# A Fourier mixing layer and an ELU feed-forward block on one core: one product, the middle x sums and the special-row copies change places

## The chip, the cores and the metric

The kernel runs on one core of one Trainium2 chip. The metric is the time of one execution on the device in microseconds, lower is better. The engines that matter are TensorE (PE in the profile; PEld is its weight load), VectorE (DVE), ScalarE (ACT), GpSimd (POOL), and SyncE (SP), which here only issues DMAs.

## The reference

```python
def _attn_ref(x, filt_r, filt_i):            # x: 8 x 3008 x 256
    X = np.fft.rfft(x, axis=1)
    F = (filt_r + 1j * filt_i)[None, :, :]   # 1505 x 256
    return np.fft.irfft(X * F, n=x.shape[1], axis=1)

def _moe_ref(x, w_in, w_out):                # 24064 x 256, 256 x 2048, 2048 x 256
    h = x @ w_in
    g = np.where(h > 0.0, h, np.exp(np.minimum(h, 0.0)) - 1.0)
    return g @ w_out
```

The output of the first, as 24064 rows, is the input of the second. All is in 32-bit floats; the filters and weights arrive as 64-bit floats.

## The kernel before

The transform of 3008 = 47 x 64 is done as matmuls with tables. Each batch goes through five stages: x sums and first transform (`x_unit` L216, `a_unit` L226: chunks c = 0 to 5, two chunks to one `a_unit`, result z written to DRAM by `z_write` and read back by `z_read`), second transform (`b_unit` L374, for groups g = 0, 2, 4, 6), product with the filter (`re_mult`, `re_sums`, `im_mult` L415, `im_join` L421, `im_sums` L425), back transform (`bi_unit`, `y_write` to DRAM) and last transform (`y_read`, `n_unit`). The feed-forward block takes the result in 6 column blocks of a batch; for each block it goes through 4 quarters of the hidden width. One such quarter is called a quad: 8 x 6 x 4 = 192 quads, of about 13 us each.

A quad holds seven up steps (products with `w_in`, a Strassen-like scheme, so that seven products do the work of eight, with sums on VectorE between them) and the seven down steps (products with `w_out`) of the quad before. An up step writes into PSUM tiles called phs, pha and phd. The second phd product of a quad (`s4`) adds onto the bank that VectorE has to read first (`s7`: `add` at L538). After these come the exponential on ScalarE (`elu_exp`, L547 and L548) and the maximum on VectorE (`elu_max`, L552).

The mixing of batch b runs beside the feed-forward block of batch b - 1, in its 24 quads, counted 0 to 23 in this text. A dictionary `plan` says which function is called in which quad, and at one of three places: place 2 behind the third step of the quad, place 0 behind the eighth (or seventh), place 1 at the quad's end, behind the sums that close its up and down steps. Each engine works off its own instructions in the order in which these calls issue them. TensorE's order of up (U) and down (D) steps is `UUDUDDU` + place 0 + `DUUDUDD`, and, for quads in the set `opens`, `DUUDUDDU` + place 0 + `DUUDUD`: the quad then begins with a down step. `opens` holds the quads behind a unit that has taken all four shared PSUM banks.

These four banks (list `banks`) go round among all stages: a unit takes the first of the list, and returns it when its readers have been issued. `b_unit` takes four, called c, s, ci and si in it, and returns them in the order c, si, s, ci. ScalarE copies c and si into tile r (L387); for group 0 it also copies one special row group of all four banks, 32 partitions x 256, into a spare filter buffer (L390); VectorE then forms sums and differences with s and ci (L392, L393).

In the order before, the plan puts: `x_unit` and `a_unit` of chunks 0 and 1, 2 and 3, 4 and 5 into quads 0, 2 and 4 (batch 1: 2, 3 and 4), sums at place 0, matmuls, copies, the loads of later chunks (`x_load`) and `z_write` at place 1; `f_read` of two groups at quads 4, 8, 12, 16, place 1, and `z_read` at quads 5, 9, 13, 17, place 0; `b_unit` at the end of quads 6, 10, 14, 18; the real products in the quad behind it, the four imaginary products one quad later at place 2 and `im_join` at that quad's end; `im_sums` and `bi_unit` in the quad behind that. Last transforms (`n_unit`) lie in quads 23, 1, 5, 8, 12, 16; the tables and y for the one of quad 5 are read at quad 3, place 0. Output sums of a block (`c_unit`, `o_unit`, L628, L651) lie in quads 1 and 2, 5 and 6, and so on to 21 and 22.

The chunks' tiles rotate: x in four buffers, their sums (`sd`, L219) in two, the result of the first transform (`t1`, L237) in three.

Of the kernel before, what the change touches and what calls it, by code (L numbers as in the profile page):

```python
# [14 lines left out]
ALU = mybir.AluOpType  # L15
# [115 lines left out]
def kernel(  # L131
# [9 lines left out]
    nc = tc.nc  # L141
# [6 lines left out]
    def pool(name, bufs, **kw):  # L148
        return ctx.enter_context(tc.tile_pool(name=name, bufs=bufs, **kw))
# [42 lines left out]
    def bank(name, shape=(P, 2, D)):  # L192
        i = banks.pop(0)
        return i, psM.tile(list(shape), FP32, tag="m%d" % i, name=name)
# [179 lines left out]
    def b_unit(b, g):  # L374

        pf = [bank("pf") for _ in range(4)]
        both = [(a, p, slice(1 if g == a == 0 else 0, 2), 0) for a in range(4) for p in range(4)]
        if g == 0:
            both = [(0, p, slice(0, 1), 1) for p in range(4)] + both
        for a, p, js, v in both:  # L380
            r = slice(32 * p, 32 * p + 24)
            nc.tensor.matmul(pf[p][1][32 * a:32 * a + 32, js, :], fb[r, v, :], t2[r, js, a, :],  # L382
                             start=True, stop=True, tile_position=(32 * p, 32 * a))
        t = rs[b, g] = sp.tile([P, 4, 2, D], FP32, tag="r", name="r")
        c, s, ci, si = (ps for _, ps in pf)
        for k, ps in ((1, c), (3, si)):
            nc.scalar.activation(out=t[:, k], in_=ps, func=AXT.Copy)  # L387
        if g == 0:
            for k, ps in ((0, c), (2, si), (1, s), (3, ci)):
                nc.scalar.activation(out=once_in[0:32, k], in_=ps[0:32, 0, :], func=AXT.Copy)  # L390
        for k, ps in ((0, s), (2, ci)):
            nc.vector.tensor_tensor(out=t[:, k], in0=t[:, k + 1], in1=ps, op=ALU.add)  # L392
            nc.vector.tensor_tensor(out=t[:, k + 1], in0=t[:, k + 1], in1=ps, op=ALU.subtract)  # L393
        banks.extend(pf[p][0] for p in (0, 3, 1, 2))
# [17 lines left out]
        if g == 0:  # L412
            nc.gpsimd.tensor_copy(out=z[0:32, 0:2, 0, :], in_=z[0:32, 2:4, 0, :])

    def im_mult(b, g, c):  # L415
        t, f = rs[b, g], fall[:, 0:2]
        nc.vector.tensor_tensor(out=t[:, c], in0=t[:, c], in1=f[:, :, 1, c, :], op=ALU.mult)
        nc.vector.tensor_tensor(out=t[:, 2 + c], in0=t[:, 2 + c], in1=f[:, :, 0, c, :], op=ALU.mult)  # L418

    def im_join(b, g):  # L420
        t = rs[b, g]  # L421
# [355 lines left out]
    with tc.manual_schedule():  # L777
# [108 lines left out]
        op = pool("op", 1)  # L886
# [9 lines left out]
        def at(quad, place, fn, *a):  # L896
            plan.setdefault((quad, place), []).append((fn, a))
# [13 lines left out]
        for b in range(B):  # L911
            t = (b - 1) * PER
            if b > 0:
                for c, s in enumerate((2, 2, 3, 3, 4, 4) if b == 1 else (0, 0, 2, 2, 4, 4)):
                    at(t + s, 0, x_unit, b, c)
                    if c % 2 == 0:
                        opens.add(t + s + 1)
                        at(t + s, 1, a_unit, b, c)
                    nb, nxt = (b, c + XBUFS) if c + XBUFS < NXC else (b + 1, c + XBUFS - NXC)
                    if nb < B:  # L920
                        at(t + s, 1, x_load, nb, nxt)
                    at(t + s, 1, z_write, b, c)
                for g in range(0, NG, 2):
                    s = t + 6 + 2 * g
                    opens.update((s + 1, s + 4))
                    for k in (g, g + 1):
                        at(s - 2, 1, f_read, b, k)
                        at(s - 1, 0, z_read, b, k)
                    at(s, 1, b_unit, b, g)
                    at(s + 1, 2, re_mult, b, g)  # L930
                    at(s + 1, 1, re_sums, b, g)
                    for c in range(2):
                        at(s + 2, 2, im_mult, b, g, c)
                    at(s + 2, 1, im_join, b, g)
                    at(s + 3, 2, im_sums, b, g)
                    at(s + 3, 1, bi_unit, b, g)
                    at(s + 3, 1, y_write, b, g)
            for m, (s, place) in enumerate(((23, 0), (25, 1), (29, 1), (32, 0), (36, 0), (40, 0))):
                if b > 0 or m > 0:
                    at(t + s - 2, 0, tn_read, b, m)  # L940
                    at(t + s - 2, 1 if m == 0 else 0, y_read, b, m)
                    at(t + s, place, n_unit, b, m)

                    at(*((t + s + 1, 1) if m > 2 else (t + s, place)), n_sums, b, m)
                at(t + PER + 4 * m + 5, 0, c_unit, b, m)
                at(t + PER + 4 * m + 6, 0, o_unit, b, m)

        items = [(b, m, q) for b in range(B) for m in range(6) for q in range(4)]
        for i in range(-PER, len(items) + 3):
# [3 lines left out]
            for n, k in enumerate("DUUDUDDU" if i in opens else "UUDUDDU"):  # L953
                s = ups if k == "U" else downs
# [7 lines left out]
            for k in "DUUDUD" if i in opens else "DUUDUDD":  # L962
                s = ups if k == "U" else downs
# [40 lines left out]
```

## Time and profile before

| what | value |
|---|---|
| median of 3 runs | 2607.95 us (2606.2 to 2610.34) |
| the profiled execution | 2609.69 us |
| its span | 2607.9 us |
| its granted TensorE clock | 0.991 |
| first product of the first quad | 100.4 us from the start |
| chain that ended last: TensorE's share | 89% |

Times in the profile are microseconds from the span's start. A timeline line gives start, duration, engine, source line, operation, output and inputs with their shapes, and how many instructions were merged; in brackets the idle time before it and what ended it. Matmul rows overlap, so that distances between starts say more than durations. A line of the list of waits gives who waited for whom, the sum, the number of times and the longest.

How work lies in the quads 0 to 5 of one batch (each of about 13 us; busy us of each engine in the stretch, with the number of instructions; then the granted clock, the share of the DMA engines and GB/s):

```profile
core 0: us, PE busy (x) PEld busy (x) DVE busy (x) ACT busy (x) POOL busy (x), PEclk, DMA share, GB/s
1054.00:1067.00 13.00, 13.00 (x87) 12.55 (x80) 7.44 (x16) 8.13 (x16) 0.00 (x0) 1.00 0.69 183
1067.00:1080.00 13.00, 12.12 (x79) 11.24 (x82) 12.60 (x25) 7.06 (x13) 0.00 (x0) 1.00 0.18 33
1080.00:1092.00 12.00, 12.00 (x78) 11.46 (x71) 4.85 (x10) 7.01 (x14) 4.41 (x9) 1.00 0.86 204
1092.00:1104.00 12.00, 12.00 (x75) 10.78 (x77) 10.37 (x18) 8.27 (x15) 0.00 (x0) 1.00 0.51 129
```

The second of these stretches is nearly quad 2, the third nearly quad 3, the fourth nearly quad 4.

### The profile page before, as it was taken

The numbers are of one execution on the slowest core, as the hardware profiler recorded it, in microseconds if no ns is written. First come the engines' busy times: TensorE is split into PE (matmuls) and PEld (weight loads), VectorE is DVE, ScalarE is ACT, GpSimd is POOL, SyncE is SP. The second block draws the span as 40 slices with busy tenths as digits, with TensorE's granted clock in tenths as the row PEclk, the third lists the DMA queues.
The fourth block names the chain that finished last, engine by engine and source line by source line (L and its number), as shares of the span: only waits on it lengthen the run. The fifth ranks groups of instructions, "written<-read, shape, count | busy, mean of one in ns | idle before, by whom it ended". The sixth has DMA issues, their size and how long they took to land.

```text
span 2607.9 us, 39668 instructions
## 1 busy us (share of the span) xinstructions
PE 2549.2 (98%) x14460; PEld 2204.1 (85%) x14460; DVE 2046.0 (78%) x3538; ACT 1546.1 (59%) x2713; POOL 169.6 (7%) x333
## 2 busy tenths in 40 slices
PE   6799999999999999999999999999999999999998
PEld 4688889888898888988889888888888888898887
DVE  6878886788867888778876888778887688866666
ACT  7665655666556655665556556565655655555554
POOL 5100100010000000000000000000010001000000
PEclk8899999999999999999999999999999999999999
DMA  9663213422243231433215231243223322120010
GB/s 275 179 173 73 69 30 96 124 69 58 52 117 93 57 77 46 114 83 75 63 41 145 68 86 37 74 124 85 57 49 81 85 65 69 36 50 20 21 29 17
DMA packets 228834, 206.37 MB, mean 79 GB/s; under 512 B 130962, under 2 KB 194674, under 8 KB 228640
## 3 DMA queue, kind: packets, MB, share of 16 engines
q1 hardware_dynamic: 211328, 166.87, 26.2%
q0 software_dynamic: 15856, 36.25, 5.1%
q8 instruction: 114, 1.87, 0.3%
q10 hardware_dynamic: 1456, 0.72, 0.1%
q14 instruction: 80, 0.66, 0.1%
HBM read 131.87 MB, written 78.17 MB: 81 GB/s over the span
## 4 chain that ended last, share of the span: by engine, by line
PE 89%; DVE 6%; DMA 2%; ACT 1%; issue 1%; POOL 0%; DVEq 0%; ACTq 0%; POOLq 0%
PE po L612 41%; PE phs L530 23%; PE phd L530 12%; PE pha L530 6%; PE psn L479 3%; PE psa L233 1%; PE pf L382 1%; PE pv L445 1%; DVE g L538 1%; DVE g L552 1%; DMA fd<-in_filt_i_dram 1%; DMA t<-in_moe_w_out_dram 0%; ACT e L548 0%; ACT e L547 0%; DMA fd<-in_filt_r_dram 0%
## 5 line engine op out<-in xcount | busy, mean ns | idle before, releaser
L612 PE MATMUL po<-g,wo 128*128 128x256 f32 (+1 forms) x5376 | 1313.0, 376 | 0.0
L612 PEld LDWEIGHTS po<-g,wo 128*128 128x128 f32 x5376 | 1012.1, 190 | 163.2 <-issue 47.4
L541 ACT ACTIVATE g<-phs 128x512 f32<-128x512 f32 (+1 forms) x576 | 338.9, 588 | 766.9 <-PE phs L530 766.9
L538 DVE TENSOR_TENSOR g<-phd,g 128x512 f32<-128x512 f32 (+1 forms) x384 | 259.5, 676 | 302.9 <-ACT e L548 205.4
L548 ACT ACTIVATE e<-e 128x512 f32<-128x512 f32 (+1 forms) x768 | 477.2, 621 | 24.4
L530 PE MATMUL phs<-y,wi 128*128 128x256 f32 (+1 forms) x1536 | 388.8, 376 | 0.5
L530 PE MATMUL phs<-ys,wi 128*128 128x256 f32 (+1 forms) x1536 | 387.7, 375 | 1.5 <-ACT g L541 1.5
L552 DVE SCALAR_TENSOR_TENSOR g<-e,g 128x512 f32<-128x512 f32 (+1 forms) x576 | 386.9, 672 | 0.8 <-ACT e L548 0.2
L547 ACT ACTIVATE e<-g 128x512 f32<-128x512 f32 (+1 forms) x576 | 353.4, 614 | 48.7 <-DVE g L538 37.0
L530 PEld LDWEIGHTS phs<-ys,wi 128*128 128x128 f32 x1536 | 291.4, 190 | 35.4 <-ACT g L541 2.5
L530 PEld LDWEIGHTS phs<-y,wi 128*128 128x128 f32 x1536 | 287.6, 190 | 38.6 <-ACT fall L390 3.4
L552 DVE SCALAR_TENSOR_TENSOR g<-e,phs 128x512 f32<-128x512 f32 (+1 forms) x192 | 129.7, 676 | 138.5 <-ACT e L548 138.5
L530 PE MATMUL phd<-ys,wi 128*128 128x256 f32 (+1 forms) x768 | 195.3, 377 | 10.0 <-DVE g L538 10.0
L530 PE MATMUL phd<-y,wi 128*128 128x256 f32 (+1 forms) x768 | 193.7, 375 | 0.0
L530 PE MATMUL pha<-y,wi 128*128 128x256 f32 (+1 forms) x768 | 193.7, 375 | 0.0
L547 ACT ACTIVATE e<-phs 128x512 f32<-128x512 f32 (+1 forms) x192 | 113.0, 588 | 125.3 <-PE phs L530 125.2
L530 PEld LDWEIGHTS phd<-ys,wi 128*128 128x128 f32 x768 | 144.6, 190 | 31.6 <-DVE g L538 15.5
L530 PEld LDWEIGHTS pha<-y,wi 128*128 128x128 f32 x768 | 145.8, 190 | 16.5
L530 PEld LDWEIGHTS phd<-y,wi 128*128 128x128 f32 x768 | 145.8, 190 | 16.5
L323 POOL DMA_DIRECT2D fall<-fp x224 | 110.5, 501 | 702.6 <-DVE r L418 650.2
L538 DVE TENSOR_TENSOR g<-pha,g 128x512 f32<-128x512 f32 (+1 forms) x192 | 129.1, 672 | 25.2 <-PE pha L530 25.1
L592 DVE TENSOR_TENSOR g<-g,g 128x512 f32<-128x512 f32 (+1 forms) x192 | 130.7, 681 | 6.7
(138 smaller groups left out, 2117.2 us busy)
## 6 DMA issues: line engine op xcount, KB each, us to landing
yd<-t SPq DMA_DIRECT2D x127, 192.0 KB
t<-yd SPq DMA_DIRECT2D x190, 128.0 KB
z<-t SPq DMA_DIRECT2D x84, 256.0 KB
fall<-fp POOLq DMA_DIRECT2D x224, 96.0 KB, 2.9
t<-z SPq DMA_DIRECT2D x224, 96.0 KB
out_dram<-o SPq DMA_DIRECT2D x632, 32.0 KB
tn<-tn_t SPq DMA_DIRECT2D x48, 256.0 KB
xc<-in_x_dram SPq DMA_DIRECT2D x84, 128.0 KB
```

What stands on the lines that cost most here:

```text
L233: nc.tensor.matmul(p[o:o + 64, u, :], w[r, u, o:o + 64], src[r, u, :], start=True, stop=True)
L323: nc.gpsimd.dma_start(t[32 * a:32 * a + 24].rearrange("p c u d -> p (c u d)"), fp[g, a].rearrange("q c u d -> q (c u d)"))
L382: nc.tensor.matmul(pf[p][1][32 * a:32 * a + 32, js, :], fb[r, v, :], t2[r, js, a, :], start=True, stop=True, tile_position=(32 * p, 32 * a))
L479: nc.tensor.matmul(ps[:, ts(q, P)], t[:, i - 4 * m, ds(dh * P, P)], w[:, i - 4 * m, :], start=True, stop=True)
L530: nc.tensor.matmul(ps[:, a, 0:h], w_in[q][:, COMBO[n], a, :], y[n], start=start and a == 0, stop=True, skip_group_check=True)
L538: nc.vector.tensor_tensor(out=g[o], in0=i0, in1=i1, op=ALU.add)
L541: nc.scalar.activation(out=g[o], in_=i0, func=AXT.Copy)
L547: nc.scalar.activation(out=e, in_=src, func=AXT.Relu, scale=-1.0)
L548: nc.scalar.activation(out=e, in_=e, func=AXT.Exp, scale=-1.0)
L552: nc.vector.scalar_tensor_tensor(out=g[n], in0=es[n], scalar=1.0, in1=src, op0=ALU.subtract, op1=ALU.max)
L592: nc.vector.tensor_tensor(out=g["t4"], in0=g["b21"], in1=g["t2"], op=ALU.subtract)
L612: nc.tensor.matmul(po[i][:, u, 0:h], w_out[q][:, COMBO[n], a, :], g[n][:, a, :], start=q == 0 and a == 0 and n in (1, 3, 6, 4), stop=True, ...
```

## The change

Three things change places; no instruction is added or removed.

1. For batches 2 to 7 the middle pair of chunks (2 and 3) moves from quad 2 to quad 3: its x sums, its matmuls and copies, its loads and its writes of z. The quad that begins with a down step because of it is 4 and no longer 3.
2. In `b_unit` the special-row copies of group 0 stand behind the copy of their own bank: c, special c, special s, si, special si, special ci, where before both full copies came first and then the special ones of c, si, s and ci.
3. `im_mult` takes the products it is to do as a list. For group 6 the last of the four moves from place 2 of its quad (quad 20) to place 1, its end, just ahead of `im_join`. For the other groups nothing moves.

```diff
-        for k, ps in ((1, c), (3, si)):
+        def keep(k, ps):
             nc.scalar.activation(out=t[:, k], in_=ps, func=AXT.Copy)
-        if g == 0:
-            for k, ps in ((0, c), (2, si), (1, s), (3, ci)):
+
+        def special(k, ps):
+            if g == 0:
                 nc.scalar.activation(out=once_in[0:32, k], in_=ps[0:32, 0, :], func=AXT.Copy)
+
+        keep(1, c)
+        special(0, c)
+        special(1, s)
+        keep(3, si)
+        special(2, si)
+        special(3, ci)
...
-    def im_mult(b, g, c):
+    def im_mult(b, g, *parts):
         t, f = rs[b, g], fall[:, 0:2]
-        nc.vector.tensor_tensor(out=t[:, c], in0=t[:, c], in1=f[:, :, 1, c, :], op=ALU.mult)
-        nc.vector.tensor_tensor(out=t[:, 2 + c], in0=t[:, 2 + c], in1=f[:, :, 0, c, :], op=ALU.mult)
+        for c, h in parts:
+            k = 2 * h + c
+            nc.vector.tensor_tensor(out=t[:, k], in0=t[:, k], in1=f[:, :, 1 - h, c, :], op=ALU.mult)
...
-                for c, s in enumerate((2, 2, 3, 3, 4, 4) if b == 1 else (0, 0, 2, 2, 4, 4)):
+                for c, s in enumerate((2, 2, 3, 3, 4, 4) if b == 1 else (0, 0, 3, 3, 4, 4)):
...
-                    for c in range(2):
-                        at(s + 2, 2, im_mult, b, g, c)
+                    parts = ((0, 0), (0, 1), (1, 0), (1, 1))
+                    early = 3 if g == 6 else 4
+                    at(s + 2, 2, im_mult, b, g, *parts[:early])
+                    at(s + 2, 1, im_mult, b, g, *parts[early:])
                     at(s + 2, 1, im_join, b, g)
```

## The prediction

> **What bounds the kernel now.** I read the share of each engine first, then the waits, then the timeline of TensorE around every break in its stream.
>
> ```profile
> PE 2549.2 (98%) x14460; PEld 2204.1 (85%) x14460; DVE 2046.0 (78%) x3538; ACT 1546.1 (59%) x2713; POOL 169.6 (7%) x333
> ```
>
> TensorE is busy for 98% of the span, so only what breaks its stream can be won. In the list of waits its breaks after the first 100 us are few:
>
> ```profile
> PE phd L530 <- DVE g L538: 10.0, 14, 0.9
> ...
> PEld phs L530 <- ACT fall L390: 3.4, 7, 0.5
> ```
>
> Fourteen waits for VectorE's sum L538 and seven for the special-row copies L390. The timeline puts them, in every batch, into three places: quad 2 (batches 2 to 7), quad 7 and quad 20 (batches 1 to 7; quads counted from the batch's start); the fourteenth wait is in quad 3 of batch 1. One batch shows all three. A group of four matmul rows of 224 columns follows the last after 0.757 us, of 256 columns after 0.863 us. Quad 2, TensorE and then VectorE:
>
> ```profile
> 1074.73 0.92 PE L612 MATMUL po<-g,wo 128*128 128x224 f32 x4
> 1076.53 1.02 PE L530 MATMUL phd<-ys,wi 128*128 128x224 f32 x4 [0.88 <-DVE g L538]
> 1077.39 1.68 PE L612 MATMUL po<-g,wo 128*128 128x224 f32 x8
> ...
> 1073.24 0.65 DVE L219 TENSOR_TENSOR sd<-xc 128x512 f32<-128x512 f32 x1
> ...
> 1075.25 0.69 DVE L220 TENSOR_TENSOR xc<-xc 128x512 f32<-128x512 f32 x1
> 1075.86 0.62 DVE L538 TENSOR_TENSOR g<-phd,g 128x448 f32<-128x448 f32 x1
> ```
>
> The second phd group was due at 1074.73 + 0.757 = 1075.49 and began at 1076.53: 1.04 late. The group after it came 0.86 later where 0.757 is usual: each break costs another 0.10 of restart. So 1.15 us. The cause stands below: L538 could not start before the four x sums, 2.62 us from 1073.24 to 1075.86. Quad 6 to 7, TensorE, ScalarE, VectorE:
>
> ```profile
> 1132.72 1.13 PE L612 MATMUL po<-g,wo 128*128 128x256 f32 x4
> 1133.92 1.13 PE L530 MATMUL phs<-y,wi 128*128 128x256 f32 x4
> 1134.89 1.03 PE L530 MATMUL pha<-y,wi 128*128 128x256 f32 x4
> 1132.54 1.08 ACT L387 ACTIVATE r<-pf 128x512 f32<-128x512 f32 x2 [0.92 <-PE pf L382]
> 1133.51 1.16 ACT L390 ACTIVATE fall<-pf 32x256 f32<-32x256 f32 x4
> 1134.44 0.69 DVE L392 TENSOR_TENSOR r<-r,pf 128x512 f32<-128x512 f32 x1 [0.28 <-ACT fall L390]
> ```
>
> The phs group needs the bank of c, which two copies read: the first L387 and the first L390, ended at 1133.51 + 0.36 = 1133.87. The phs group was due at 1133.68 (0.863 and the 0.10 restart after 1132.72): 0.24 late, and 0.10: 0.345 us. Quad 20, and the same sum in quad 21:
>
> ```profile
> 1312.49 1.03 PE L612 MATMUL po<-g,wo 128*128 128x256 f32 x4
> 1314.10 1.13 PE L530 MATMUL phd<-ys,wi 128*128 128x256 f32 x4 [0.58 <-DVE g L538]
> 1315.07 1.89 PE L612 MATMUL po<-g,wo 128*128 128x256 f32 x8
> ...
> 1312.76 0.68 DVE L418 TENSOR_TENSOR r<-r,fall 128x512 f32<-128x512 f32 x1
> 1313.36 0.69 DVE L538 TENSOR_TENSOR g<-phd,g 128x512 f32<-128x512 f32 x1
> ...
> 1324.83 0.69 DVE L538 TENSOR_TENSOR g<-phd,g 128x512 f32<-128x512 f32 x1
> ```
>
> Due at 1313.35, begun at 1314.10: 0.745 and 0.10, 0.85 us, behind four products of 0.60 each. In all 6 x 1.15 + 7 x 0.345 + 7 x 0.85 = 15.2 us of breaks: the most that this change can win.
>
> **Part 1, the middle x sums and their matmuls one quad later** (batches 2 to 7). No instruction is added. Quad 2 loses 2.62 us of VectorE work ahead of L538. That sum then starts when its matmul ends, near 1074.2; TensorE's next group started 0.74 after the sum's start in quad 20, and with 0.10 of restart it is ready at 1075.1, due at 1075.49. The wait goes: -1.15 each, -6.9 us.
> What quad 3 gets: VectorE was busy for 4.85 of the 12 us from 1080 to 1092, so the 2.62 us fit. Step by step, with the first break gone: VectorE's tail of quad 2 ends near 1080.6, the pha sum and four x sums end near 1083.9, and the phd matmuls (quad 3 now in the order without a leading down step) end at about 1084.7. VectorE is 0.8 early; TensorE's margin there is the usual 0.4. Cost 0; were this wrong by the whole, it would be a break like batch 1's in quad 3 (0.63 idle, 0.9 in all, with four weight sums besides the x sums), 5.4 us.
> Quad 4 now begins with a down step, has its own four x sums and its own first-transform matmuls behind. Batch 1 already runs quad 4 in just that order, without a break. The 32 psa rows (1079.00 to 1080.89, and 0.50 of mode changes) cost the same at the end of quad 3. Their four banks are those of the quad before, as at the end of quad 2 now.
> Queues: SP issues up to 18 transfers for the two chunks (loads of the next chunks, writes of z; 1082.07 to 1092.95). They now stand behind the table read and four y reads of quad 3, which were issued from 1093.0 to 1096.2 and come about 11 us earlier: nothing waits for them before 1117. On POOL the memset L211 waits for these matmuls (130.1 us in this batch), and behind it stand the eight f reads L323, issued from 1080.7 to 1084.6. All move about 10 us; their tile is read in quad 7, at 1138. They overlap the same z writes as before.
> The tight one is tile t1, three buffers: chunk 5's copy at the end of quad 4 takes the buffer of chunk 2, whose z write will be issued a quad later. Now it is issued at 1084.9 and 1085.5 and the later half lands at 1091.5, 6 us after, with the DMA engines full. Moved, it is issued near 1093 and lands near 1099.5; the copy comes at about 1104. Cost 0, with 4.5 us in hand; ends: 0 and, with 8 us more of landing, 3.5 us per batch, 21 us.
>
> **Part 2, special copies behind their own bank's copy** (group 0 only, seven times). ScalarE's starts lie 0.48 apart behind a full copy and 0.265 behind a special one. New order from 1132.54: copy c, special c 1133.02, special s 1133.28, copy si 1133.55, special si 1134.03, special ci 1134.29. Bank c is free at 1133.38 in place of 1133.87; with 0.05 of semaphore and 0.10 of restart the phs group is ready at 1133.53, due at 1133.68. The break goes: -0.345, -2.4 us. The pha group takes bank si, free at 1134.39 to 1134.42 (before: 1134.14), ready at 1134.54 to 1134.57, and due at 1134.55: up to 0.03 late, 0.2 us in all; I take 0. The ends are 0 and one special copy, 0.265 x 7 = 1.9 us of the 2.4 given back.
> L392 ended its wait with the third L390, special s. That is a wait of one reader of a bank for another reader. The Trainium skill, "PSUM — Partial Sum Buffer", section "PSUM bank collisions raise a hardware error", says that two engines may not touch one bank and one group of 32 partitions at once, reading included. By that rule the sum stays behind special s, which is third in both orders; with a wait for its own operand alone it would never have idled. By the rule VectorE gains 0.37 us here, without it nothing; on TensorE's sum both make 0.
> VectorE's own row: special s ends at 1133.65, so L392 starts when VectorE is free, 1134.07 for 1134.44: 0.37 earlier, as TensorE is 0.345 earlier. Nothing is late next: in quad 7 VectorE idles 1.23 us before its phd sum.
>
> **Part 3, the last product of group 6 moved behind quad 20** (seven times). L538 in quad 20 starts 0.60 earlier, 1312.76; TensorE's group at 1313.50, 0.15 late, and 0.10: 0.25 left of 0.85. TensorE comes 0.60 earlier into quad 21, but VectorE doesn't: the elu step of b12 still waits for ScalarE's exponential (ended 1314.49), so its next steps gain only 0.05, 0.16 and 0.29, and the tail of quad 20 ends 0.29 earlier. Then the moved product takes its 0.60. The work behind it is 0.31 later: two joins, pha sum, two im sums and two output sums, and L538 of quad 21 starts at 1324.97 (VectorE was free for it at 1324.66 and it began at 1324.83, with its matmul). TensorE's group is then ready at 1324.97 + 0.74 + 0.10 = 1325.81, due at 1326.29 - 0.60 = 1325.69: 0.12 late. Won: 0.60 - 0.12 = 0.48 each, 3.3 us (3.36). Ends: the tail of quad 20 gains nothing, 0.29 later again, 0.19 won and 1.3 us; and the whole 0.85, 5.9 us.
>
> **Sum.** 6.9 + 2.4 + 3.3 = 12.6 us. The profiled execution took 2609.69 us with a span of 2607.9: it becomes 2597.1. It stands 1.74 above the median of the runs shown, 2607.95, so the median becomes 2595.3. TensorE has no other break before the end, so what is won in a batch stays won.
>
> **Rivals.**
> (a) Part 3 pays itself back in quad 21 and part 2's break moves to the pha group. For it: the margins are 0.1 us and less. Against it: ScalarE's starts are regular to 0.01. Gain 6.9 + 0.5 + 1.3 = 8.7: 2599.3.
> (b) The x sums break quad 3 as they break quad 2. For it: batch 1's quad 3 has such a break. Against it: there VectorE has four weight sums more, here 7 us idle. 6.9 - 5.4 leaves 1.5 of part 1: gain 7.2, 2600.8.
> (c) The wait for t1 (other side): chunk 2's z write lands behind the f reads, ScalarE stands in order before chunk 5's copy, and TensorE lacks banks. Equal to before when the landing takes 6 + 4.5 + 12.6/6 = 12.6 us; with 14 us, 3.5 x 6 = 21 us lost, 8.4 slower: 2616.4. Against it: z writes under full DMA engines took 6 us.
> (d) No measurable change: two of the parts do not take effect, or the breaks return elsewhere, about 2605.
>
> **How the numbers follow.** Chances: my forecast 0.64, its own range 2592.0 to 2597.5; (a) 0.16; (b) 0.10; (d) 0.06; (c) 0.04. A measurement of this kernel tells about 0.2% (5.2 us) from no change: faster 0.90, same 0.06, slower 0.04. The range ends below at all breaks gone, 2607.95 - 15.2 = 2592.7, less 2 for the spread of the runs (2606.2 to 2610.34): 2590.7; above it takes in (a) and (b), 2601.0.
>
> **What would show it.** In the changed trace: no break in quad 2, none in quads 3 and 4; seven waits of phs for L390 gone; in quad 20 an idle time below 0.2 before the second phd group, and a short break in quad 21; from one batch's first psa row to the next's (1052.79 and 1367.54, 314.75 us) 1.15 + 0.345 + 0.48 less, 312.8 us. Wrong would show as ScalarE waiting for z writes before psa copies, or VectorE's L538 late in quads 3 or 21.

## The result, and the profile after

The changed kernel takes 2596.25 us (median of 6 runs, 2594.98 to 2597.56) against 2608.33 us before (2605.86 to 2610.79, also 6, with the three shown above among them): 12.1 us or 0.49% less, ratio 0.9951 with a 95% interval of 0.9940 to 0.9962. Forecast were 2595.3 us and 12.6 us less.

The profiled execution took 2595.51 us with a span of 2593.7 us, 14.2 us less than the one before. That is more than the medians' difference, and the surplus is not of the change: the first product of the first quad began at 98.97 us, not 100.39, and the first quad was 0.2 us shorter. In the ten profiled executions of this study, one of each kernel, that first product began anywhere from 96.3 to 102.7 us. This may be most of the spread of the runs, but only the profiled ones show it. From there on the batches of one trace repeat to 0.01 or 0.02 us. The clock is not the cause either: 0.991 was granted before and 0.992 after, and matmul rows of 256 columns follow each other after 0.216 us in both. I therefore compare the distance from one batch's first psa row (the first transform's first matmul row) to the next's, for batches 4 and 5 throughout. In TensorE's timeline, before and then after:

```profile
1052.79 0.43 PE L233 MATMUL psa<-sd,ta 64*64 64x256 f32 x2
...
1367.54 0.43 PE L233 MATMUL psa<-sd,ta 64*64 64x256 f32 x2
```

```profile
1046.44 0.43 PE L233 MATMUL psa<-sd,ta 64*64 64x256 f32 x2
...
1359.23 0.43 PE L233 MATMUL psa<-sd,ta 64*64 64x256 f32 x2
```

After: 1359.23 - 1046.44 = 312.79 us; before: 1367.54 - 1052.79 = 314.75. So 1.96 us less in each of the six batches that have all three parts, where 1.15 + 0.345 + 0.48 = 1.975 were forecast. With batch 1, which has parts 2 and 3 alone, the change is worth 6 x 1.96 + 0.81 = 12.6 us.

The lines of source move by up to 9 from `b_unit` on: L538 of before is L547, L552 is L561, L390 is L391, L418 is L427. In the list of TensorE's waits the fourteen of matmuls for VectorE's sum have become one, batch 1's quad 3. The list counts a matmul's wait only where the matmuls before it had ended; the weight loads, which stand idle sooner, still wait for that sum sixteen times, fourteen of them in quads 20 and 21:

```profile
PE phd L539 <- DVE g L547: 0.6, 1, 0.6
...
PEld phd L539 <- DVE g L547: 5.7, 16, 1.0
```

No weight load waits for a special-row copy any more, where seven did.

Quad 2 after, VectorE and then TensorE:

```profile
1065.65 1.30 DVE L660 STREAM_TRANSPOSE o<-c 128x512 f32<-128x512 f32 x2
1067.89 0.62 DVE L547 TENSOR_TENSOR g<-phd,g 128x448 f32<-128x448 f32 x1 [0.93 <-PE phd L539]
```

```profile
1068.38 0.92 PE L621 MATMUL po<-g,wo 128*128 128x224 f32 x4
1069.13 0.92 PE L539 MATMUL phd<-ys,wi 128*128 128x224 f32 x4
1069.89 1.68 PE L621 MATMUL po<-g,wo 128*128 128x224 f32 x8
```

Behind the transposes VectorE now idles 0.93 us until the phd matmuls end, and TensorE's groups follow at the usual 0.76. Quad 3, which has the x sums now:

```profile
1076.88 0.69 DVE L220 TENSOR_TENSOR xc<-xc 128x512 f32<-128x512 f32 x1
1078.48 0.62 DVE L547 TENSOR_TENSOR g<-phd,g 128x448 f32<-128x448 f32 x1 [0.92 <-PE phd L539]
```

It idles 0.92 there; I had put that at 0.8. The z write of chunk 2, in two halves, and then ScalarE's copies of chunks 4 and 5, the last of which takes that chunk's buffer:

```profile
1086.07 1.25 SPq L307 DMA_DIRECT2D z<-t  x2
```

```profile
1097.06 2.04 ACT L237 ACTIVATE t<-psa 128x512 f32<-128x512 f32 x4
```

The copies have no idle time before them. Quad 6 to 7, ScalarE, TensorE, VectorE:

```profile
1125.53 0.62 ACT L391 ACTIVATE fall<-pf 32x256 f32<-32x256 f32 x2
1126.06 0.58 ACT L387 ACTIVATE r<-pf 128x512 f32<-128x512 f32 x1
1126.53 0.63 ACT L391 ACTIVATE fall<-pf 32x256 f32<-32x256 f32 x2
```

```profile
1125.21 1.13 PE L621 MATMUL po<-g,wo 128*128 128x256 f32 x4
1126.18 1.03 PE L539 MATMUL phs<-y,wi 128*128 128x256 f32 x4
1127.04 1.04 PE L539 MATMUL pha<-y,wi 128*128 128x256 f32 x4
1127.92 0.81 PE L621 MATMUL po<-g,wo 128*128 128x256 f32 x3
```

```profile
1126.56 0.68 DVE L400 TENSOR_TENSOR r<-r,pf 128x512 f32<-128x512 f32 x1
```

The phs group begins 0.97 behind the down step, on time. The pha group takes 0.88 to the next where 0.863 is usual: 0.016 late. L400 (L392 before) starts with no idle time. Quads 20 and 21, TensorE and VectorE:

```profile
1304.66 1.03 PE L621 MATMUL po<-g,wo 128*128 128x256 f32 x4
1305.66 1.13 PE L539 MATMUL phd<-ys,wi 128*128 128x256 f32 x4
...
1316.98 1.03 PE L621 MATMUL po<-g,wo 128*128 128x256 f32 x4
1317.87 1.13 PE L539 MATMUL phd<-ys,wi 128*128 128x256 f32 x4
```

```profile
1306.68 0.69 DVE L561 SCALAR_TENSOR_TENSOR g<-e,phs 128x512 f32<-128x512 f32 x1 [0.48 <-ACT e L557]
...
1312.07 0.75 DVE L637 TENSOR_TENSOR c<-po,k 128x256 f32<-128x256 f32 x2
1312.74 0.68 DVE L427 TENSOR_TENSOR r<-r,fall 128x512 f32<-128x512 f32 x1
...
1317.13 0.68 DVE L547 TENSOR_TENSOR g<-phd,g 128x512 f32<-128x512 f32 x1
```

Quad 20: 1305.66 is 0.14 behind 1304.66 + 0.863, and 0.10 of restart, 0.24 in all. Quad 21: 1317.87 is 0.02 late, and 0.10, 0.13. In quad 20 VectorE stands idle for 0.48 us before the maximum that reads phs (that of the tile called b12), for the exponential. The same maximum, and the last output sums of the quad, before:

```profile
1314.56 0.68 DVE L552 SCALAR_TENSOR_TENSOR g<-e,phs 128x512 f32<-128x512 f32 x1
...
1320.20 0.74 DVE L628 TENSOR_TENSOR c<-po,k 128x256 f32<-128x256 f32 x2
```

Counted from TensorE's down step ahead of the break (1312.49 before, 1304.66 after), VectorE's first phd sum starts 0.61 us earlier than before, the maximum of b12 only 0.05, and the output sums 0.29 by the unrounded times.

### The profile page after: what moved, and what is told of

Same layout as the page of the kernel before. It is cut to its first block, busy times and chain, and to the rows that moved or that the text cites. A ratio compares the mean times of both kernels' runs of the same rounds, so it can differ in the third digit from the quotient of the medians.

```text
span 2593.7 us, 39657 instructions
## 1 busy us (share of the span) xinstructions
PE 2545.1 (98%) x14460; PEld 2200.3 (85%) x14460; DVE 2043.7 (79%) x3538; ACT 1547.5 (60%) x2713; POOL 169.2 (7%) x333
## 4 chain that ended last, share of the span: by engine, by line
PE 96%; DMA 2%; DVE 1%; ACT 0%; issue 0%; SPq 0%; DVEq 0%; ACTq 0%
PE po L621 44%; PE phs L539 25%; PE phd L539 13%; PE pha L539 6%; PE psn L488 3%; PE psa L233 1%; PE pf L382 1%; PE pv L454 1%; DMA xc<-in_x_dram 1%; DMA x<-in_x_dram 0%; DMA yd<-t 0%; PE po L329 0%; PE po L295 0%; PE psa L276 0%; DMA t<-yd 0%
## 5 line engine op out<-in xcount | busy, mean ns | idle before, releaser
L550 ACT ACTIVATE g<-phs 128x512 f32<-128x512 f32 (+1 forms) x576 | 338.9, 588 | 754.7 <-PE phs L539 753.3
L547 DVE TENSOR_TENSOR g<-phd,g 128x512 f32<-128x512 f32 (+1 forms) x384 | 259.3, 675 | 293.6 <-ACT e L557 206.8
L561 DVE SCALAR_TENSOR_TENSOR g<-e,g 128x512 f32<-128x512 f32 (+1 forms) x576 | 386.7, 671 | 0.3 <-ACT e L557 0.2
L561 DVE SCALAR_TENSOR_TENSOR g<-e,phs 128x512 f32<-128x512 f32 (+1 forms) x192 | 129.8, 676 | 141.3 <-ACT e L557 140.9
L547 DVE TENSOR_TENSOR g<-pha,g 128x512 f32<-128x512 f32 (+1 forms) x192 | 128.9, 672 | 23.2 <-PE pha L539 23.1
```

Source lines behind the costliest of these rows:

```text
L547: nc.vector.tensor_tensor(out=g[o], in0=i0, in1=i1, op=ALU.add)
L550: nc.scalar.activation(out=g[o], in_=i0, func=AXT.Copy)
L561: nc.vector.scalar_tensor_tensor(out=g[n], in0=es[n], scalar=1.0, in1=src, op0=ALU.subtract, op1=ALU.max)
```

## The experiments

The distance of a batch in each run, from one trace each; the times given for e1 to e7 are single executions, that for e8 a median of 5.

| run | distance, us | against (base) |
|---|---|---|
| before | 314.75 | |
| after | 312.79 | -1.96 |
| e1, part 1 alone | 313.60 | -1.15 (before) |
| e2, part 2 alone | 314.42 | -0.33 (before) |
| e3, part 3 alone | 314.30 | -0.45 (before) |
| e4, x sums stay in quad 2 | 313.96 | +1.17 (after) |
| e5, two products at the end | 313.39 | +0.60 (after) |
| e6, special s behind special si | 312.86 | +0.07 (after) |
| e7, product in the gap | 312.66 | -0.13 (after) |
| e8, both gaps | 312.42 | -0.37 (after) |

The theory: three separate breaks, each won by its own part, and in part 3 VectorE's work is lent to quad 21 and not saved. The rivals: that the parts need one another, that the moved matmuls and transfers are part of the gain, that the breaks only move.

### e1: part 1 alone

```diff
-                for c, s in enumerate((2, 2, 3, 3, 4, 4) if b == 1 else (0, 0, 2, 2, 4, 4)):
+                for c, s in enumerate((2, 2, 3, 3, 4, 4) if b == 1 else (0, 0, 3, 3, 4, 4)):
```

> Part 1 alone. If the three breaks of TensorE are separate and part 1 takes its own (1.15 us in quad 2 of batches 2 to 7), the distance from one batch's first product to the next is 314.75 - 1.15 = 313.60 us, quad 2 has no break, quads 7 and 20 keep theirs (0.345 and 0.85). If the parts need one another (the sum of VectorE's work in a batch decides), less than 0.8 of it shows. If the x sums only carry the break into quad 3, 314.75 stays and quad 3 waits for L538.

313.60 us, 1.15 less; 2603.59 us. No break is left in quad 2 and none has come in quad 3. TensorE's two breaks in quads 7 and 20 are 0.24 and 0.745 with their 0.10, as before.

### e2: part 2 alone

```diff
-        for k, ps in ((1, c), (3, si)):
...
-        if g == 0:
-            for k, ps in ((0, c), (2, si), (1, s), (3, ci)):
...
+        keep(1, c)
+        special(0, c)
+        special(1, s)
+        keep(3, si)
+        special(2, si)
+        special(3, ci)
```

> Part 2 alone. Separate breaks: 314.75 - 0.345 + at most 0.03 = 314.41 to 314.44 us a batch, the wait of the phs group in quad 7 gone, the pha group behind it up to 0.03 late. If the break only moves to the pha group: up to 314.67.

314.42 us, 0.33 less; 2603.64 us. That single time can't be read against 2612.05 us of the kernel before on the same chip: the first product began at 96.3 us in this execution, the earliest of all. The phs group is on time, the pha group 0.016 late.

### e3: part 3 alone

`im_mult` takes its products as a list, as in the change; in the plan:

```diff
-                    for c in range(2):
-                        at(s + 2, 2, im_mult, b, g, c)
+                    parts = ((0, 0), (0, 1), (1, 0), (1, 1))
+                    early = 3 if g == 6 else 4
+                    at(s + 2, 2, im_mult, b, g, *parts[:early])
+                    at(s + 2, 1, im_mult, b, g, *parts[early:])
```

> Part 3 alone. Separate breaks: quad 20's falls from 0.85 to 0.24 and quad 21 gets one of 0.12 to 0.13: 314.75 - 0.48 = 314.27 us a batch. If part 3 owes something to the other two parts (VectorE less loaded before it), it is less: 314.5 or more.

314.30 us, 0.45 less; 2606.78 us. Quad 20 is 0.14 late and quad 21 0.03, each with 0.10. The three parts alone add up to 1.15 + 0.33 + 0.45 = 1.93 of the 1.96: no more than 0.04 us (by the unrounded distances) hangs on their being together.

### e4: the x sums stay in quad 2, the rest moves

```diff
-                    at(t + s, 0, x_unit, b, c)
+                    at(t + (2 if b > 1 and c in (2, 3) else s), 0, x_unit, b, c)
```

> The changed kernel, but the four middle x sums stay in quad 2; only the matmuls, copies, loads and z writes of chunks 2 and 3 go to quad 3. If VectorE's 2.62 us ahead of L538 is the whole cause, quad 2's break is back in full: 312.79 + 1.15 = 313.94 us a batch. If the place of the matmuls, their copies and their transfers, or which quad begins with a down step, is part of the gain, 312.79 to 313.5.

313.96 us: 1.17 more than after, the whole of part 1's gain. TensorE's timeline in quad 2:

```profile
1073.42 0.92 PE L539 MATMUL phd<-y,wi 128*128 128x224 f32 x4
...
1076.74 1.02 PE L539 MATMUL phd<-ys,wi 128*128 128x224 f32 x4 [0.89 <-DVE g L547]
```

Moving the matmuls, copies, loads, z writes and the leading down step is worth nothing by itself, to 0.02 us. VectorE's four sums are the cause.

### e5: two products at quad 20's end

```diff
-                    early = 3 if g == 6 else 4
+                    early = 2 if g == 6 else 4
```

> The changed kernel with two products of group 6, not one, at quad 20's end. If VectorE's work has only been lent to quad 21: quad 20 has no break (won 0.85 against the kernel before), L538 of quad 21 starts another 0.60 later while TensorE comes 0.25 earlier, so that quad 21's break grows from 0.12 to about 0.97: 312.79 - 0.24 + 0.85 = 313.40 us a batch. If quad 21 has room that the working overlooked, 312.55.

313.39 us, as the account of lent work had it (313.40). Quad 20 has no break any more, quad 21 a large one:

```profile
1310.27 1.03 PE L539 MATMUL phd<-ys,wi 128*128 128x256 f32 x4
...
1323.22 1.13 PE L539 MATMUL phd<-ys,wi 128*128 128x256 f32 x4 [0.70 <-DVE g L547]
```

VectorE in quad 20:

```profile
1311.43 0.69 DVE L561 SCALAR_TENSOR_TENSOR g<-e,phs 128x512 f32<-128x512 f32 x1 [1.08 <-ACT e L557]
```

The maximum of b12 starts 1311.43 - 1051.19 = 260.24 us behind the batch's first psa row, as in the changed kernel (1306.68 - 1046.44), although VectorE was free for it 0.60 us sooner: the exponential holds it. So moving more of the same work along is worse than none at all: 0.96 lost in quad 21 for 0.85 won in quad 20. Of none, one and two products, one is the best number for this place.

### e6: special s behind special si

```diff
-        special(1, s)
         keep(3, si)
         special(2, si)
+        special(1, s)
```

> The changed kernel with special s behind special si (order: c, special c, si, special si, special s, special ci). If L392, which reads bank s on VectorE, waits for ScalarE's special copy of that bank although both only read, it starts at about 0.31 us later than in the changed kernel, 0.02 to 0.04 behind the end of special s, the fifth copy; TensorE's pha group finds its bank earlier and its 0.016 goes: 312.77 us a batch. If L392 waits for its own operand alone, it starts where it does in the changed kernel.

312.86 us, and not 312.77. The first half of the expectation came true: VectorE's sum on bank s waits for ScalarE's copy of the same bank, though both only read it (special s, the fifth copy, ended at 1129.485, and L400 began 0.03 later). VectorE:

```profile
1129.52 0.69 DVE L400 TENSOR_TENSOR r<-r,pf 128x512 f32<-128x512 f32 x1 [0.28 <-ACT fall L391]
```

Against the copies' start it begins at 1129.52 - 1127.62 = 1.90 us, against 1126.56 - 1125.04 = 1.52 in the changed kernel: 0.37 later, where I had said 0.31. The pha group's 0.016 is gone, but another break came that I had not foreseen. ScalarE, then TensorE:

```profile
1132.34 1.06 ACT L408 ACTIVATE r<-fall 32x1024 f32<-32x1024 f32 x1 [1.91 <-DVE r L401]
1133.30 0.57 ACT L550 ACTIVATE g<-phs 128x512 f32<-128x512 f32 x1
```

```profile
1132.21 1.89 PE L621 MATMUL po<-g,wo 128*128 128x256 f32 x8
1133.94 1.11 PE L539 MATMUL phs<-ys,wi 128*128 128x256 f32 x4
1134.89 1.03 PE L621 MATMUL po<-g,wo 128*128 128x256 f32 x4
```

The late sums hold back L408, the copy of the special rows, which waits for the last of them; behind it in ScalarE's order stands the copy L550, and the next phs matmuls add onto the bank which that copy reads. The copy ended at 1133.87; with 0.05 us to hand over (as from 1133.87 to 1133.92 in quad 7 before) and 0.10 of restart the group is ready at 1134.02, where it was due at 1133.94. It takes 0.08 us longer (1134.89 - 1133.94 = 0.95, usual 0.863). The weight loads of such phs groups wait for L550 eleven times in this run and four times in the changed kernel, seven more, one for each batch from 1 to 7:

```profile
PEld phs L539 <- ACT g L550: 4.2, 11, 1.2
```

I had looked at who waits for L392 and not at what is queued behind the one who waits.

### e7: the product in VectorE's gap

A fourth place is added to the plan, behind the second step of the quad's second half, which is the one with the first maximum; the moved product goes there.

```diff
-            for k in "DUUDUD" if i in opens else "DUUDUDD":
+            for n, k in enumerate("DUUDUD" if i in opens else "DUUDUDD"):
...
+                if n == 1:
+                    for fn, a in plan.get((i, 3), ()):
+                        fn(*a)
...
-                    at(s + 2, 1, im_mult, b, g, *parts[early:])
+                    at(s + 2, 3, im_mult, b, g, *parts[early:])
```

> The changed kernel with the moved product not at quad 20's end but behind quad 20's first maximum (L561 of b11), where VectorE stands idle about 0.55 us for ScalarE's exponential. Quad 20 keeps 0.24, quad 21 loses its 0.12 to 0.13: 312.79 - 0.125 = 312.67 us a batch. If the gap is not free (what follows in quad 20 comes 0.6 later), quad 21 keeps its break: 312.79.

312.66 us, 0.13 less than after. VectorE in quad 20:

```profile
1305.04 0.68 DVE L561 SCALAR_TENSOR_TENSOR g<-e,g 128x512 f32<-128x512 f32 x1
1305.63 0.68 DVE L427 TENSOR_TENSOR r<-r,fall 128x512 f32<-128x512 f32 x1
1306.24 0.68 DVE L561 SCALAR_TENSOR_TENSOR g<-e,phs 128x512 f32<-128x512 f32 x1
```

The product fills the hole of 0.48 us seen above and delays what follows by about 0.05 (the maximum of b12 starts 1306.24 - 1045.95 = 260.29 us behind the batch's first psa row, where it was 260.24). Quad 21 has no break any more, quad 20 keeps 0.24.

### e8: both gaps

The fourth place of e7 stands here too.

```diff
-                                    (3, 0, w_sums, 15)):
+                                    (3, 3, w_sums, 15)):
...
-                    early = 3 if g == 6 else 4
+                    early = 2 if g == 6 else 4
...
-                    at(s + 2, 1, im_mult, b, g, *parts[early:])
+                    at(s + 2, 3, im_mult, b, g, *parts[early:early + 1])
+                    at(s + 2, 1, im_mult, b, g, *parts[early + 1:])
...
-                at(t + PER + 4 * m + 5, 0, c_unit, b, m)
+                at(t + PER + 4 * m + 5, 3 if m == 4 and b < B - 1 else 0, c_unit, b, m)
```

> The changed kernel with two products taken out of quad 20's first half: one into the gap behind the first maximum, one to the quad's end; in quad 21 the two output sums that stand ahead of L538 go into the same gap there; and in batch 1 the four weight sums of quad 3 go there too. By the account of VectorE's time all breaks of quads 20 and 21 go (0.24 + 0.125 = 0.37 us a batch): 312.42 us a batch, and batch 1's quad 3 loses its 0.9: 7 x 0.37 + 0.9 = 3.5 us less than the changed kernel, about 2592.8 by the median of runs. If VectorE's work is only moved about, 312.8 and 2596.

312.42 us a batch, as expected: no break is left in quads 20 and 21. Time 2594.73 us (median of 5, 2593.24 to 2596.51), beside 2609.11 us for the kernel before (9 runs), ratio 0.9944, interval 0.9931 to 0.9958. It is ahead of the kernel before; against the changed kernel (0.9951) the intervals overlap, and only the distance in the trace, 0.37 us a batch, tells them apart. The median expected was 2592.8, 1.9 us less: 0.33 of that is accounted for below, and the rest is within the spread of the runs. In batch 1 quad 3 the break before the second phd group is gone, but the quad became only 0.57 us shorter (13.58 to 13.01), not 0.9. VectorE and TensorE there:

```profile
143.41 0.42 DVE L755 TENSOR_TENSOR wo<-wo 128x256 f32<-128x256 f32 x1
143.74 0.61 DVE L561 SCALAR_TENSOR_TENSOR g<-e,phs 128x448 f32<-128x448 f32 x1
```

```profile
143.93 0.43 PE L233 MATMUL psa<-sd,ta 64*64 64x256 f32 x2
...
146.15 1.02 PE L621 MATMUL po<-g,wo 128*128 128x224 f32 x4
```

From the first psa row to the next down step it takes 2.22 us; in quads 2 and 4 of that batch it takes 1.89. The weight sums hold back the maximum that reads bank s, and the sum behind it that reads the next, until after the psa rows have begun, which need these banks for their second half. The 0.33 fits that, but no run shows that these sums alone cause it; which of the two banks it was, the trace doesn't say.

## Why the prediction was right

- **Part 1**, -1.15 a batch: the break is gone in the changed kernel and in e1, in that size; e4 shows that the four sums alone cause it. VectorE's margin in quad 3 was 0.92 for 0.8.
- **Part 1's transfers**, cost 0: the z write of chunk 2 was issued at 1086.07, where I had said 1093 (that figure was worked out from the time of the profile before, which stood 6 us later at this batch); its later half landed at 1093.34 by the trace's semaphore counts, 6.6 us after that half's issue, and the copies of the last pair began at 1097.06, chunk 5's about 1 us later. ScalarE never waited for it: of rival (c) nothing is seen. The margin was 4.7 us for 4.5. That 8 us more of landing would cost what I had said was not tried.
- **Part 2**, -0.345: measured 0.33, the rest being the 0.016 of the pha group, for which 0 to 0.03 had been left. The reader does wait for the reader: e6 moved the one and the other followed at 0.03 us. That agrees with the rule of the Trainium skill, "PSUM — Partial Sum Buffer", section "PSUM bank collisions raise a hardware error", that two engines must be kept off one bank and one group of 32 partitions at the same time, two readers included. The working calls special s third in both orders; it was the third special copy and the fifth copy of all before, and is the second special copy and the third of all after, and its times were reckoned for that.
- **Part 3**, -0.48: 0.24 was left in quad 20 (0.25 forecast) and 0.13 came in quad 21 (0.12). The step that mattered was not the 0.60 of the product but that the exponential of b12 fixes VectorE's next start, so that only 0.29 of it came through to the quad's end; 0.05 at b12 and 0.29 at the end were forecast, and measured. e5 doubles the product and finds the loan and its repayment to 0.01 us; e7 finds the gap that this wait leaves.
- **Sum**, 12.6 us forecast, 12.6 by the distances, 12.1 by the medians. Rival (a) stayed within the forecast: the pha group pays back 0.016 and quad 21 0.13, where (a) had 0.27 and 0.41. (b) and (d) are not seen. That the median came within 1 us of the forecast is in part luck, for the runs of one kernel spread over 2.6 us and more; the distances in the traces are the evidence.

What let the working come out so near, as I read it, is that each of these waits ends with one instruction whose start repeats from batch to batch to 0.01 or 0.02 us. Where I left part of such a chain out (e6), I was wrong in the sign.

## What to carry to other kernels

When one engine is busy for 98%, list its breaks one by one, and for each the work that stands ahead of the releasing instruction: that work's duration, minus the slack, is the prize, and it can be moved to where the same engine idles, if nothing stands behind it there that the first engine needs soon (the weight sums of e8 fill such a gap, and 0.33 us came back behind them). Work put off to the end of a stage is lent, not saved: follow the lending engine until it next idles, for a wait of its own on the way (here an exponential) sets how much comes back. Where an instruction gets later, look also at what is queued behind the one that waits for it.

## What I had not expected of the hardware

The first 100 us, in which the tables, weights and x arrive, differ by up to 6.4 us between the ten profiled executions (first product at 96.3 to 102.7 us), while each later batch repeats to 0.01 or 0.02 us; so a quarter of a microsecond a batch can be told from the trace and 2 us not from a single time. A break of TensorE costs 0.10 us beside its wait, even where the wait is 0.02 us long (quad 21 after): the first row after it takes 0.32 us to the next in place of 0.216. Where the wait ends just before the group is due, only a part of the 0.10 shows: 0.016 in the pha group after, 0.08 in e6.
